# v times p of two pairs in one run, five p buffers, and the third W_out tile behind the attention units

## The chip, the cores and the metric

The kernel runs on one core of a Trainium2 chip. The metric is device microseconds of one execution. Its engines are TensorE (PE, matmuls; PEld is its weight load), VectorE (DVE), ScalarE (ACT), GpSimd (POOL) and SyncE (SP), whose queue issues all of this kernel's DMAs.

## What is computed

Attention with a block-causal mask (8 batches, 8 heads, 576 positions, head size 64), and behind it a feed-forward network on the 4608 tokens:

```python
scores = scale * np.matmul(q, k.transpose(0, 1, 3, 2))
scores = np.where(block_i >= block_j, scores, -1e9)          # blocks of 64
attn = np.exp(scores - scores.max(-1, keepdims=True))
attn = attn / (attn.sum(-1, keepdims=True) + 1e-09)
x = np.matmul(attn, v).transpose(0, 2, 1, 3).reshape(4608, 512)
h = x @ w_in                                                 # 512 x 2048
out = (h * (1.0 / (1.0 + np.exp(-h)))) @ w_out               # 2048 x 512
```

## The kernel before

Most products are made of fp32r pieces, a high part and a low part of each operand, three matmuls for one. v times p alone is in plain fp32, which the trace shows as two matmuls for each one in the program.

The program has three stages. In the first (to about 80 us) the weights W_in arrive as 64-bit words and are turned into numbers, and the first 128 positions of each head are attended to. In the second stage 64 **units** u0 to u63 (8 batches of 8 heads) attend to the other 448 positions, while the first layer of the network (tiles h) runs between them. In the third (from about 620 us) 72 **items** i0 to i71 carry the second layer, each as seven products of sums of blocks, with W_out in the same form.

A unit i has these steps. `load`, `split_hi` (ACT), `split_k`, `split_q` (POOL): q and k in two parts. `scores` (PE, L719): ten matmuls into three of four PSUM banks S. `max`, `gather`, `top`, `spread`, `wide` (DVE and ACT): the maximum of each row. `sub` (DVE, S minus maximum into tile T) and `exp` (ACT, T into tile p). `add` (POOL) and `sums` (DVE): row sums. For each **pair** of units, at the odd one: `sums_x`, `sums_g`, `sums_m`, `inverse` (the factor of each row), `pv` (PE, L824, v times p into PSUM tile U: five widths, two units, ten matmuls in the program and twenty in the trace), `mult` (DVE, U times the factor, into xu), `x_hi` (ACT, L833) and `x_lo` (POOL, L836): the two parts of x, which the first layer reads.

The first layer is cut into **h steps** (`ffn`, six matmuls each, L1063). Two steps fill one tile h, of which there are two buffers; `keep` (ACT, L1069) copies it to SBUF as g, and `save` (SP) writes it to DRAM, from where the items read it again. An h tile can only be begun when the keep of the tile two before it has been done. The h steps of a batch need x of all of its units.

W_out is made of eight tiles t0 to t7, each from two loads o (o0 and o1 for t0, and so on). For one tile: two `load`s into os0 and os1, two `rebias` (ACT, L531, into the tile wraw), three `bits` for each half (DVE, through PSUM bank C, back into wraw), `x` 0 to 2 (POOL, sums and differences into xs), `hi` 0 to 3 (ACT, L646) and `lo` 0 to 3 (POOL, L651). wraw, xs and C have one buffer each. Tiles t0 to t2 (NTA = 3) have room of their own in the pool `ta` and are made while the units run; t3 to t7 stand in room that the units leave free, and are made between the last unit (`all.attended`) and the items.

The order is written out by hand as a list of steps (ORDER): each engine carries out its own instructions in the order of that list, and the semaphores come from the tiles. The list is no time table; only the order on each engine counts.

The lines that the change touches:

```python
def place(u):                                    # of a W_out tile
    if u.d < NTA:
        t = pools["ta"].tile(...)
    elif u.d < 6:
        t = sp.tile([P, 2 * 7 * 256], F32R, tag=f"tb{u.d}", name="tb")
...
n = u.i % 5 if u.double else u.i % 3             # exp: which p buffer
u.p = (pools["p"] if n > 2 else sp).tile([P, COLS], F32, tag=f"p{n}", name="p")
...
for y in (units[u.i - 2], u) if u.double else (u,):       # pv
    U = y.U = (bank("C") if u.double and y is u else pU.tile(...))[:, :NQ]
    for n, (j, c, q0, w) in enumerate(SEG[i] for i in PV):
        for e, z in enumerate((y.mate, y)):
            nc.tensor.matmul(U[64 * e : 64 * e + 64, q0 : q0 + w], y.vv[:, e, j], z.p[:, c : c + w], ...)
```

Of the kernel before, what the change touches and what calls it, by code (L numbers as in the profile page):

```python
# [95 lines left out]
o2.load u0.wide u0.sub:0 u0.sub:1 u1.scores u1.max:0 t0.hi:2 o3.load o2.rebias u3.load keep o3.rebias keep u1.max:1 u0.load_v
u2.split_hi u1.max:2 u1.gather ffn o2.bits:0 u2.split_q save ffn u2.split_k u0.sub:2 u1.top o2.bits:1 t0.lo:2 u1.spread o2.bits:2
keep ffn save u0.exp:0 u1.load_v u1.wide u0.exp:2 ffn u1.sub:0 u1.sub:1 u1.exp:0 u2.scores u1.exp:1 u1.sub:2 save u1.exp:2
u2.max:0 u0.exp:1 u0.add:0 u0.add:1 u3.split_hi u3.split_k u2.max:1 u2.max:2 u2.gather u1.pv u0.sums:0 ffn o3.bits:0 ffn
u3.split_q save u2.top u0.sums:1 u2.spread u1.sums:0 u2.wide u4.load u5.load u2.sub:0 t0.hi:3 u2.sub:1 u2.exp:0 u1.add:0 keep  # L100
u1.add:1 u3.scores u2.exp:1 u4.split_hi u3.max:0 u3.max:1 ffn t0.lo:3 u2.sub:2 keep u3.max:2 u1.sums:1 u4.split_k u4.split_q
u3.gather u1.sums_x u2.exp:2 u1.sums_g u3.top o3.bits:1 ffn o3.bits:2 u3.spread u1.sums_m keep u3.wide u3.sub:0 u3.sub:2 ffn
u3.exp:0 ffn u1.inverse u6.load u2.add:0 ffn u2.add:1 ffn u3.exp:2 save u3.sub:1 u2.sums:0 u4.scores t1.x:0 u1.mult u3.exp:1
u2.sums:1 u4.max:0 u4.max:1 t1.hi:0 u3.add:0 u3.add:1 u3.sums:0 u3.sums:1 t1.hi:2 u2.load_v u3.load_v u4.max:2 keep u5.split_hi
u3.pv u3.sums_x ffn save u4.gather save o4.load t1.lo:0 keep ffn u4.top save u4.spread u4.load_v u5.split_k ffn save keep save
u6.load_v u5.split_q t1.lo:2 u7.load_v u3.sums_g u4.wide u7.load ffn u3.sums_m u4.sub:0 u4.sub:2 u4.exp:0 ffn u1.x_hi u5.load_v
u4.sub:1 u4.exp:2 keep u4.add:0 u3.inverse o5.load u4.exp:1 save u5.scores u3.mult u4.add:1 u5.max:0 u3.x_hi u4.sums:0 ffn u3.x_lo
u6.split_hi u4.sums:1 t1.hi:1 u5.max:1 t1.x:1 ffn u5.max:2 keep u6.split_k save u5.gather ffn u5.top u5.spread ffn keep u5.wide
t1.x:2 u6.split_q u8.load t1.lo:1 u5.sub:0 t1.hi:3 ffn save u5.sub:2 u5.exp:0 t1.lo:3 u5.sub:1 u5.exp:2 u6.scores keep u5.add:0
u6.max:0 u5.exp:1 save u6.max:1 o4.rebias u5.pv u5.add:1 u7.split_hi u6.max:2 u5.sums:0 u7.split_q u5.sums:1 u6.gather u6.top  # L110
u5.sums_x ffn u7.split_k o4.bits:0 u6.spread u8.load_v u9.load_v u6.wide u5.sums_g ffn u6.sub:0 u1.x_lo u9.load u5.sums_m u6.sub:2
u6.sub:1 u7.scores o5.rebias u6.exp:0 u6.exp:2 keep u7.max:0 u6.add:0 u6.exp:1 u7.max:1 save ffn u8.split_hi u6.add:1 u7.max:2 ffn
u8.split_q u5.inverse u7.gather u7.top u6.sums:0 u7.spread u8.split_k ffn u6.sums:1 keep u7.wide save u7.sub:0 ffn u10.load
u7.sub:2 u7.exp:0 u7.sub:1 u7.exp:2 u8.scores keep u8.max:0 u7.add:0 u7.exp:1 save u8.max:1 ffn u9.split_hi u5.mult u7.add:1
u7.sums:0 u7.sums:1 u7.pv u9.split_q u5.x_hi u7.sums_x u8.max:2 u7.sums_g u9.split_k o4.bits:1 u8.gather u8.top ffn u11.load
u5.x_lo o4.bits:2 u8.spread u8.wide t2.hi:0 u10.load_v u7.sums_m ffn u8.sub:0 u11.load_v keep u8.sub:2 u8.exp:0 save ffn u8.sub:1
u8.exp:2 t2.lo:0 u7.inverse u8.exp:1 u8.add:0 u9.scores u7.mult keep u9.max:0 u8.add:1 save u7.x_hi u9.max:1 ffn u10.split_hi
u7.x_lo u9.max:2 ffn u10.split_k u8.sums:0 u9.gather u8.sums:1 u9.top o5.bits:0 ffn u9.spread u10.split_q u9.wide keep ffn
u9.sub:0 save u12.load u9.sub:2 u9.exp:0 u9.sub:1 u10.scores u9.exp:2 keep u10.max:0 u9.add:0 u9.exp:1 u10.max:1 save u9.pv
u11.split_hi u10.max:2 u9.add:1 u11.split_q u9.sums:0 u10.gather u9.sums:1 u10.top u9.sums_x ffn u10.spread u11.split_k o5.bits:1  # L120
u12.load_v u9.sums_g u13.load_v u10.wide u10.sub:0 ffn u13.load u9.sums_m u10.sub:2 u10.exp:0 ffn u10.sub:1 u10.exp:2 keep
u9.inverse u10.add:0 u10.exp:1 u11.scores save u11.max:0 u10.add:1 u11.max:1 ffn u12.split_hi u11.max:2 ffn keep u12.split_q
u10.sums:0 u10.sums:1 u11.gather save u9.mult ffn u12.split_k u11.top u11.spread o5.bits:2 ffn u9.x_hi u11.wide u14.load t2.x:0
keep u11.sub:0 t2.hi:1 ffn save u11.sub:2 u11.exp:0 u9.x_lo t2.hi:2 u11.sub:1 u12.scores u11.exp:2 t2.lo:2 u12.max:0 u11.exp:1
u12.max:1 keep u11.pv u13.split_hi u11.add:0 save u11.sums:0 u12.max:2 u11.add:1 u12.gather u13.split_q u11.sums:1 ffn u14.load_v
u11.sums_x u12.top u15.load_v u12.spread u13.split_k ffn u11.sums_g u12.wide u12.sub:0 u15.load u11.sums_m ffn u12.exp:0 u12.sub:1
keep u12.sub:2 u13.scores u12.exp:1 save u13.max:0 t2.lo:1 u12.exp:2 u13.max:1 ffn u14.split_hi u12.add:0 u13.max:2 ffn keep
u12.sums:0 u11.inverse u13.gather save ffn u13.top u12.add:1 u11.mult u14.split_q u13.spread u14.split_k u11.x_hi u12.sums:1 ffn
keep u13.wide save ffn u13.sub:0 u11.x_lo u16.load u13.sub:1 u13.exp:0 u14.scores u13.sub:2 t2.x:1 u13.exp:1 u13.exp:2 u14.max:0
t2.x:2 u14.max:1 keep u13.pv u13.add:0 u15.split_hi save u14.max:2 u13.add:1 t2.hi:3 u13.sums:0 u14.gather u15.split_q ffn u14.top  # L130
u13.sums:1 u16.load_v u13.sums_x u14.spread u17.load_v u15.split_k u13.sums_g u14.wide ffn u14.sub:0 u17.load u13.sums_m u14.sub:1
u14.exp:0 u15.scores keep u15.max:0 u14.exp:1 save u15.max:1 ffn t2.lo:3 u16.split_hi u15.max:2 ffn u16.split_q u13.inverse
u15.gather u15.top ffn u15.spread u16.split_k u14.sub:2 keep ffn u14.exp:2 u13.mult u15.wide save u13.x_hi u18.load u15.sub:0
u14.add:0 ffn u15.sub:1 u15.exp:0 u13.x_lo keep u15.sub:2 u15.exp:1 u16.scores save u14.sums:0 u15.exp:2 u14.add:1 u16.max:0
u16.max:1 u15.pv u17.split_hi u14.sums:1 u16.max:2 u15.add:0 u15.sums:0 u16.gather u17.split_q ffn u18.load_v u16.top u16.spread
u19.load_v u15.add:1 u16.wide ffn keep u17.split_k u15.sums:1 save u15.sums_x ffn u16.sub:0 u15.sums_g u16.sub:1 u19.load
u16.exp:0 u15.sums_m u17.scores u16.sub:2 u16.exp:1 u16.exp:2 u17.max:0 u17.max:1 ffn keep u16.add:0 u18.split_hi save u17.max:2
u16.sums:0 ffn u16.add:1 u15.inverse u17.gather u18.split_q ffn u17.top u15.mult u17.spread keep u18.split_k u16.sums:1 ffn
u15.x_hi u17.wide save u17.sub:0 ffn u20.load u15.x_lo keep u17.sub:1 u17.exp:0 save u17.sub:2 u18.scores u17.exp:1 u18.max:0
u17.exp:2 u18.max:1 u17.add:0 u17.pv u19.split_hi u18.max:2 u17.add:1 u17.sums:0 u18.gather u19.split_q u17.sums:1 u18.top ffn  # L140
u17.sums_x u20.load_v u18.spread u19.split_k u21.load_v u17.sums_g u18.wide ffn keep u18.sub:0 u21.load u17.sums_m u18.sub:1
u18.exp:0 u19.scores u18.sub:2 save u18.exp:1 u19.max:0 u18.exp:2 ffn u19.max:1 u20.split_hi u18.add:0 u19.max:2 ffn keep
u20.split_q u18.sums:0 u19.gather save u17.inverse ffn u18.add:1 u19.top u17.mult u19.spread u20.split_k ffn u18.sums:1 keep
# [1142 lines left out]
```

## Time and profile before

| | us |
|---|---|
| median of 3 runs | 970.33 |
| lowest and highest run | 970.29, 970.47 |
| the profiled execution | 971.3 |
| its span, first to last instruction | 969.5 |

The page of the profile gives the busy time of each engine over the span, the span in 40 slices of 24.2 us, and the chain of work that ended last. A timeline lists instructions by their start; neighbours of one kind are merged into a row with a count, and a bracket at its end gives the idle time before it and what ended that. Matmuls overlap in the pipeline, so the distance of two starts is their price and not the duration in the row.

### The profile page before, as it was taken

What the parts mean: (1) busy time and instruction counts of PE and PEld (TensorE: products, weight loads), DVE (VectorE), ACT (ScalarE), POOL (GpSimd) and SP (SyncE); (2) the same over time, 40 slices, a digit from 0 to 9 for tenths busy, and PEclk for the clock granted to TensorE, in tenths of its full rate; (3) what the DMA queues carried; (4) which work ended last, traced back from release to release, by engine and by line L of the source; (5) the groups of instructions that cost most, each with busy time, mean ns of one, the idle gap of its engine ahead of it and who ended that gap; (6) DMA issues with size and microseconds to landing.
All of it is one profiled execution on the core that took longest, in us unless ns stands there. A gap on an engine that the chain in (4) does not pass through costs nothing.

```text
span 969.5 us, 20758 instructions
## 1 busy us (share of the span) xinstructions
PE 960.0 (99%) x6922; PEld 869.0 (90%) x6922; DVE 767.5 (79%) x1975; ACT 687.7 (71%) x1557; POOL 619.0 (64%) x724
## 2 busy tenths in 40 slices
PE   8999999999999999999999999999999999999998
PEld 7778778888888888888888899999999999999998
DVE  6868889899999999899999743498877787777762
ACT  5977677777777777777787645799677777677750
POOL 6566897988878778788787647655444444434440
PEclk9999999999999999999999999999999999999999
DMA  9956655555555555455555166665454454444521
GB/s 345 360 187 192 193 162 156 150 152 157 146 157 154 150 159 159 137 157 163 142 157 161 68 203 200 199 185 156 122 165 137 135 158 129 136 140 137 139 66 45
DMA packets 109803, 155.51 MB, mean 160 GB/s; under 512 B 18560, under 2 KB 83072, under 8 KB 109696
## 3 DMA queue, kind: packets, MB, share of 16 engines
q1 hardware_dynamic: 109696, 154.18, 53.6%
q8 instruction: 55, 0.90, 0.4%
q14 instruction: 52, 0.43, 0.1%
HBM read 106.95 MB, written 47.19 MB: 159 GB/s over the span
## 4 chain that ended last, share of the span: by engine, by line
PE 95%; DMA 2%; ACT 1%; DVE 1%; SPq 0%; POOL 0%; issue 0%; ACTq 0%; POOLq 0%
PE h L1063 40%; PE S L1140 25%; PE c L1140 10%; PE S L719 9%; PE U L824 9%; DMA v<-in_v_dram 2%; PE S L1004 1%; PE S L881 0%; PE S L1035 0%; ACT raw L1091 0%; DVE Mx L658 0%; POOL MR L874 0%; ACT gc L1124 0%; SPq L905 0%; PE h L853 0%
## 5 line engine op out<-in xcount | busy, mean ns | idle before, releaser
L1063 PE MATMUL h<-x,wi 128*128 128x448 f32 (+2 forms) x1968 | 416.8, 367 | 0.0
L1063 PEld LDWEIGHTS h<-x,wi 128*128 128x128 f32 x1968 | 356.8, 188 | 34.1 <-issue 0.7
L658 DVE TRANSPOSE_TENSOR_REDUCE Mx<-S 64x4 f32<-64x128 f32 (+4 forms) x384 | 130.5, 400 | 8.9 <-PE S L719 8.0
L773 ACT ACTIVATE p<-T 128x512 f32<-128x512 f32 (+1 forms) x192 | 115.0, 614 | 26.9 <-DVE T L762 20.1
L1069 ACT COPY g<-h 128x448 f32<-128x448 f32 (+1 forms) x160 | 86.3, 539 | 36.4 <-PE h L1063 22.0
L1128 POOL TENSOR_TENSOR x<-raw,x 128x512 fp32r<-128x512 f32 (+1 forms) x58 | 59.3, 1027 | 72.9 <-ACT x L1124 59.9
L779 POOL TENSOR_TENSOR pa<-p 128x448 f32<-128x448 f32 x64 | 73.7, 1151 | 43.7 <-ACT p L773 37.9
L1128 POOL TENSOR_TENSOR wi<-raw,wi 128x512 fp32r<-128x512 f32 (+1 forms) x56 | 57.3, 1027 | 67.9 <-ACT wi L1124 58.6
L700 POOL TENSOR_TENSOR qh<-qk,qh 64x576 fp32r<-64x576 f32 x64 | 91.8, 1434 | 6.4 <-POOL xs L636 0.8
L719 PE MATMUL S<-qh 128*128 128x448 f32 (+3 forms) x320 | 92.2, 301 | 0.1
L824 PE MATMUL U<-p,v 128*64 128x448 f32 (+3 forms) x640 | 87.0, 416 | 0.4 <-DMA v<-in_v_dram 0.4
L719 PE MATMUL S<-ql,qh 128*128 128x448 f32 (+3 forms) x320 | 83.9, 306 | 0.0
L694 ACT CAST qh<-qk 128x1024 fp32r<-128x1024 f32 x64 | 67.0, 1047 | 22.5 <-PE S L719 5.9
L704 POOL TENSOR_TENSOR ql<-qk,qh 128x448 fp32r<-128x448 f32 x64 | 73.7, 1151 | 14.0 <-issue 6.7
L824 PEld LDWEIGHTS U<-p,v 128*64 128x64 f32 x640 | 44.0, 136 | 41.0 <-issue 29.0
L1091 ACT ACTIVATE raw<-raw 128x1024 f32<-128x1024 f32 x72 | 76.6, 1064 | 0.0
L765 DVE TENSOR_TENSOR T<-S,MR 128x128 f32<-128x128 f32 (+2 forms) x192 | 73.4, 409 | 0.0
L719 PEld LDWEIGHTS S<-ql,qh 128*128 128x128 f32 (+1 forms) x320 | 56.9, 178 | 6.4
L719 PEld LDWEIGHTS S<-qh 128*128 128x128 f32 (+1 forms) x320 | 56.8, 178 | 3.6 <-issue 0.3
L782 POOL TENSOR_TENSOR pa<-pa,p 128x320 f32<-128x320 f32 x64 | 55.9, 874 | 5.3 <-ACT p L773 1.5
L744 ACT COPY m<-m 32x14 f32<-32x14 f32 x192 | 38.7, 202 | 23.9 <-DVE m L740 22.2
L1128 POOL TENSOR_TENSOR gc<-raw,gc 128x512 fp32r<-128x512 f32 (+1 forms) x30 | 30.8, 1031 | 37.0 <-ACT gc L1124 30.1
(198 smaller groups left out, 2065.9 us busy)
## 6 DMA issues: line engine op xcount, KB each, us to landing
qk<-in_qk_dram SPq DMA_DIRECT2D x128, 256.0 KB, 3.8
gdb<-g SPq DMA_DIRECT2D x128, 224.0 KB, 2.4
raw<-gdb SPq DMA_DIRECT2D x64, 256.0 KB, 3.2
v<-in_v_dram SPq DMA_DIRECT2D x64, 160.0 KB, 2.3
wst<-in_moe_w_in_dram SPq DMA_DIRECT2D x16, 512.0 KB, 8.4
wst<-in_moe_w_out_dram SPq DMA_DIRECT2D x16, 512.0 KB, 4.4
gd<-g SPq DMA_DIRECT2D x32, 256.0 KB, 3.7
raw<-gd SPq DMA_DIRECT2D x32, 256.0 KB, 3.5
```

Source lines behind the costliest of these rows:

```text
L658: nc.vector.tensor_reduce(out=out, in_=in_, axis=AX.X, op=op, apply_transpose=True)
L700: nc.gpsimd.tensor_tensor(out=u.qh[r, c], in0=u.raw[r, c], in1=u.qh[r, c], op=ALU.subtract)
L704: nc.gpsimd.tensor_tensor(out=u.ql, in0=u.raw[:, :NQ], in1=u.qh[:, :NQ], op=ALU.subtract)
L719: nc.tensor.matmul(u.ps(c, w, m), u.kk[r, j * P : j * P + m], q[r, q0 : q0 + w], start=qq == 0 and not (ROWS and seg == 2), stop=qq == 1 a ...
L773: nc.scalar.activation(u.p[:, c:e], u.T[:, c:e], AF.Exp, scale=SCALE)
L779: nc.gpsimd.tensor_tensor(out=u.pa, in0=u.p[:, :NQ], in1=u.p[:, 960 : 960 + NQ], op=ALU.add)
L824: nc.tensor.matmul(U[64 * e : 64 * e + 64, q0 : q0 + w], y.vv[:, e, j], z.p[:, c : c + w], start=n == 0, stop=n == 4)
L1063: nc.tensor.matmul(o, wi[wt][:, c, w], x_of(g, c, xt), start=c + k == 0, stop=c == CT - 1 and k == 2)
L1069: nc.scalar.copy(g, hs.pop(z)[:, :n])
L1091: nc.scalar.activation(u.raw, u.raw, AF.Silu)
L1128: e.tensor_tensor(out=u.goal(1, k), in0=u.source(k), in1=u.goal(0, k), op=ALU.subtract)
L1140: nc.tensor.matmul(o, quarter(u.g[a], j)[:, P * e : P * e + P], quarter(turned[d].g[b], TORDER[FACTOR[pr]]), start=u.q == 0 and i % 2 == 0 ...
```

## The change

Two constants and the order list are changed:

```diff
-NTA = 3
-DOUBLE = 0
+NTA = 2
+DOUBLE = 1
...
-u62.sub:2 u63.gather u61.inverse u62.exp:2 ffn keep u63.top u62.add:0 u61.mult u63.spread save u62.sums:0 ffn u61.x_hi u63.wide
...
+u63.exp:1 u63.add:0 u59.x_hi u63.add:1 save ffn u63.sums:0 ffn u63.sums:1 u63.sums_x keep u63.pv u61.inverse ffn u59.x_lo u61.mult
```

With DOUBLE = 1, units from u8 on rotate through five p buffers, two of them in a pool of their own that takes the place of the third tile of `ta`. pv is called for every fourth unit (u11, u15, up to u63) and carries out two pairs, the earlier one into U and the later one into bank C. Before, pv ran 32 times, once for each pair; now 4 times for one pair and 14 times for two. With NTA = 2 the tile t2 belongs to the tiles in the units' room, and stands behind `all.attended` with t3 to t7: six tiles are made there, and five were. The list is another from about the first unit to the place where t6 is finished; from there to the end (from o14, through all items) it is the same, step for step. The lines of the changed file stand one lower in number (L823 for L824, L530 for L531).

PE at the first pair of batch 1 (units u8 and u9; S are scores, U is v times p, h the first layer), before:

```order
L719 MATMUL S0_2315<-ql_2290,qh_2256 64x64
L824 MATMUL U_2337<-p_2205,v_1973 64x448
L824 MATMUL U_2337<-p_2308,v_1973 64x448
L824 MATMUL U_2337<-p_2205,v_1973 64x448
L824 MATMUL U_2337<-p_2308,v_1973 64x448
L824 MATMUL U_2337<-p_2205,v_1973 64x320
L824 MATMUL U_2337<-p_2308,v_1973 64x320
L824 MATMUL U_2337<-p_2205,v_1973 64x192
L824 MATMUL U_2337<-p_2308,v_1973 64x192
L824 MATMUL U_2337<-p_2205,v_1973 64x64
L824 MATMUL U_2337<-p_2308,v_1973 64x64
L1063 MATMUL h_2367<-x_81,wi0_78 128x448 x2
```

and PE at the same pair and the next one (u10 and u11) now; the rows begin with the end of the first pair:

```order
L823 MATMUL U_2440<-p_2242,v_2098 64x64
L823 MATMUL SC_2451<-p_2289,v_2200 64x448
L823 MATMUL SC_2451<-p_2406,v_2200 64x448
L823 MATMUL SC_2451<-p_2289,v_2200 64x448
L823 MATMUL SC_2451<-p_2406,v_2200 64x448
L823 MATMUL SC_2451<-p_2289,v_2200 64x320
L823 MATMUL SC_2451<-p_2406,v_2200 64x320
L823 MATMUL SC_2451<-p_2289,v_2200 64x192
L823 MATMUL SC_2451<-p_2406,v_2200 64x192
L823 MATMUL SC_2451<-p_2289,v_2200 64x64
L823 MATMUL SC_2451<-p_2406,v_2200 64x64
L1062 MATMUL h_2492<-x_81,wi0_78 128x448 x2
```

The second pair follows the first without scores or h between them.

ACT at the end of the last unit (p is the last exp, g are keeps, x is x_hi, wraw is a rebias, dj belongs to the row sums), before:

```order
L1069 COPY g_7757<-h_7717 128x448
L667 COPY dj_7771<-dj_7771 32x28 x3
L1069 COPY g_7797<-h_7763 128x448
L1069 COPY g_7818<-h_7790 128x448
L833 CAST x_81<-xu_7809 128x448
L1069 COPY g_7844<-h_7811 128x448
L1069 COPY g_7860<-h_7837 128x448
L531 ACTIVATE wraw_7862<-wst_7833 128x512
L1069 COPY g_7881<-h_7853 128x448
L531 ACTIVATE wraw_7862<-wst_7835 128x512
L646 CAST tb_7894<-wraw_7862 128x256
```

and now:

```order
L832 CAST x_81<-xu_7710 128x448
L1068 COPY g_7739<-h_7721 128x448
L666 COPY dj_7737<-dj_7737 32x28 x3
L832 CAST x_81<-xu_7774 128x448
L832 CAST x_81<-xu_7800 128x448
L530 ACTIVATE wraw_7820<-wst_7816 128x512
L1068 COPY g_7825<-h_7766 128x448
L530 ACTIVATE wraw_7820<-wst_7818 128x512
L645 CAST tb_7854<-wraw_7820 128x256
```

The first rebias (now o4's, then o6's) stands right behind the last x_hi, where two keeps stood between them. On PE the last run of v times p stands four h steps later in the program than it did.

ACT at the rebias of o12, the first of the tile t6 (tb are hi of t5, then wi0 is hi of t6), before:

```order
L1069 COPY g_8132<-h_8108 128x448
L646 CAST tb_8089<-xs_8104 128x512
L531 ACTIVATE wraw_8151<-wst_8087 128x512
L1069 COPY g_8154<-h_8125 128x448
L1069 COPY g_8174<-h_8144 128x448
L531 ACTIVATE wraw_8151<-wst_8106 128x512
L646 CAST wi0_78<-wraw_8151 128x256
```

and now:

```order
L1068 COPY g_8107<-h_8088 128x448
L530 ACTIVATE wraw_8141<-wst_8080 128x512
L645 CAST tb_8082<-xs_8105 128x512
L1068 COPY g_8147<-h_8112 128x448
L530 ACTIVATE wraw_8141<-wst_8109 128x512
L645 CAST tb_8082<-xs_8105 128x512
L1068 COPY g_8159<-h_8128 128x448
L645 CAST wi0_78<-wraw_8141 128x256
```

The two casts of t5 now stand behind the rebias, and each has a keep behind it.

## Rows read from the trace of the kernel before

**Rows 1.** The page: busy time of the engines, the granted TensorE clock in 40 slices (tenths of full speed), and the shares of the chain that ended last.

```profile
PE 960.0 (99%) x6922; PEld 869.0 (90%) x6922; DVE 767.5 (79%) x1975; ACT 687.7 (71%) x1557; POOL 619.0 (64%) x724
...
PEclk9999999999999999999999999999999999999999
...
PE 95%; DMA 2%; ACT 1%; DVE 1%; SPq 0%; POOL 0%; issue 0%; ACTq 0%; POOLq 0%
```

**Rows 2.** Who waited for whom, PE alone, the whole span: us in total, times, longest. These two are the only ones behind the first stage.

```profile
PE U L824 <- DMA v<-in_v_dram: 0.4, 1, 0.4
PE S L1140 <- DVE x L1128: 0.4, 1, 0.4
```

**Rows 3.** Timeline of PE at pairs in the middle of the units (start, us, engine, line, operation, tiles, shape, count); each row is of an answer for a stretch so narrow that it shows single matmuls.

```profile
301.72 2.57 PE L1063 MATMUL h<-x,wi 128*128 128x448 f32 x12
304.12 0.36 PE L719 MATMUL S<-qh 128*128 128x448 f32 x1
...
305.47 0.22 PE L719 MATMUL S<-ql,qh 128*64 128x64 f32 x1
305.62 0.60 PE L824 MATMUL U<-p,v 128*64 128x448 f32 x2
306.05 0.55 PE L824 MATMUL U<-p,v 128*64 128x448 f32 x2
306.42 0.55 PE L824 MATMUL U<-p,v 128*64 128x448 f32 x2
306.80 0.55 PE L824 MATMUL U<-p,v 128*64 128x448 f32 x2
...
308.05 0.28 PE L824 MATMUL U<-p,v 128*64 128x64 f32 x3
308.10 0.22 PE L824 MATMUL U<-p,v 128*64 128x64 f32 x1
308.25 0.48 PE L1063 MATMUL h<-x,wi 128*128 128x448 f32 x1
308.57 0.36 PE L1063 MATMUL h<-x,wi 128*128 128x448 f32 x1
...
312.13 0.22 PE L719 MATMUL S<-ql,qh 128*64 128x64 f32 x1
312.19 0.45 PE L1063 MATMUL h<-x,wi 128*128 128x448 f32 x1
312.48 0.57 PE L1063 MATMUL h<-x,wi 128*128 128x448 f32 x2
```

**Rows 4.** Timelines of PE, DVE, ACT, POOL and SP at the end of the last unit, and the page's row on the loads of W_out (issues, KB of each, median us from issue to landing).

```profile
552.24 2.70 PE L824 MATMUL U<-p,v 128*64 128x448 f32 x20
554.88 11.47 PE L1063 MATMUL h<-x,wi 128*128 128x448 f32 x56
...
559.48 0.62 DVE L828 TENSOR_TENSOR xu<-U,MR 128x448 f32<-128x448 f32 x1
...
560.59 0.57 ACT L833 CAST x<-xu 128x448 fp32r<-128x448 f32 x1
...
565.26 0.67 ACT L531 ACTIVATE wraw<-wst 128x512 f32<-128x512 f32 x1
...
wst<-in_moe_w_out_dram SPq DMA_DIRECT2D x16, 512.0 KB, 4.4
```

**Rows 5.** Timelines of ACT, DVE and POOL along W_out tiles behind the units: t5 from its first rebias to the first one of t6, then the end of t6 and the first rebias of t7.

```profile
586.86 1.23 ACT L531 ACTIVATE wraw<-wst 128x512 f32<-128x512 f32 x2
587.57 0.69 DVE L554 TENSOR_SCALAR SC<-wraw 128x512 uint32<-128x512 uint32 x1 [6.97 <-ACT wraw L531]
591.35 0.69 DVE L564 SCALAR_TENSOR_TENSOR wraw<-wst,SC 128x512 uint32<-128x512 uint32 x1
592.18 1.29 POOL L632 TENSOR_TENSOR xs<-wraw 128x512 f32<-128x512 f32 x1 [1.14 <-DVE wraw L564]
595.06 1.29 POOL L651 TENSOR_TENSOR tb<-wraw,tb 128x512 fp32r<-128x512 f32 x1
596.39 0.67 ACT L531 ACTIVATE wraw<-wst 128x512 f32<-128x512 f32 x1 [0.63 <-POOL tb L651]
...
605.92 0.62 ACT L646 CAST wi<-xs 128x512 fp32r<-128x512 f32 x1 [1.72 <-POOL xs L636]
606.45 0.53 ACT L1069 COPY g<-h 128x448 f32<-128x448 f32 x1
606.87 1.23 ACT L531 ACTIVATE wraw<-wst 128x512 f32<-128x512 f32 x2
```

**Rows 6.** Timelines of POOL and PE where the items begin.

```profile
619.59 2.01 POOL L1128 TENSOR_TENSOR gc<-raw,gc 128x512 fp32r<-128x512 f32 x2 [0.71 <-ACT gc L1124]
...
620.99 1.58 PE L1140 MATMUL S<-ta,gc 128*128 128x256 f32 x12
...
628.37 0.39 PE L1140 MATMUL S<-ta,x 128*128 128x256 f32 x2
629.12 0.38 PE L1140 MATMUL S<-ta,x 128*128 128x256 f32 x1 [0.35 <-DVE x L1128]
```

**Rows 7.** Busy time by engine in stretches (us; PE, PEld, DVE, ACT, POOL with their instructions; granted clock, DMA share, GB/s).

```profile
300.00:450.00 150.00, 150.00 (x864) 128.44 (x863) 138.26 (x411) 111.44 (x286) 120.72 (x154) 1.00 0.54 151
...
575.00:600.00 25.00, 25.00 (x127) 23.43 (x126) 10.85 (x16) 13.76 (x26) 16.91 (x17) 1.00 0.58 176
```

More of the change, by code (lines that the diff above doesn't have):

```diff
@@ L96 @@
[L96 to L143, printed above, removed]
@@ L148 @@
-keep u19.inverse u21.gather save u22.split_q ffn u19.mult u21.top u20.sums:0 u21.spread u22.split_k u20.sums:1 ffn u19.x_hi
-u21.wide keep u24.load u19.x_lo u21.sub:0 ffn u21.sub:1 u21.exp:0 save u21.sub:2 u22.scores u21.exp:1 u21.exp:2 u22.max:0
-u22.max:1 keep u21.pv u21.add:0 u23.split_hi save u22.max:2 u21.add:1 u21.sums:0 u22.gather u23.split_q u21.sums:1 ffn u22.top
-u21.sums_x u24.load_v u22.spread u23.split_k u25.load_v u21.sums_g u22.wide ffn u22.sub:0 u25.load u21.sums_m u22.sub:1 u22.exp:0
@@ new lines @@
+u16.add:0 ffn u15.sums_m u17.sub:2 u18.top u18.spread keep u15.inverse u16.sums:0 u19.split_k u13.x_hi u11.x_lo save u19.split_q
+u18.wide ffn u16.add:1 u18.sub:0 u15.mult save u17.exp:0 u17.exp:1 u18.sub:1 u19.scores ffn u15.x_hi keep u13.x_lo u17.exp:2
+u21.load u18.sub:2 u19.max:0 u17.load_v u16.sums:1 ffn u20.split_hi keep u19.max:1 u19.max:2 u15.x_lo u19.gather u20.split_k
+u19.top u19.spread u20.split_q u18.exp:0 u19.wide u19.sub:0 u18.exp:1 u19.sub:2 ffn u19.sub:1 ffn ffn u20.scores u19.exp:0
@@ new lines @@
+u20.add:1 ffn u23.top keep ffn u24.split_k u19.inverse u23.spread u22.load_v u22.exp:2 ffn u21.sums:0 save u23.wide u23.sub:0
+u24.split_q u23.sub:2 u23.sub:1 u20.sums:1 u19.mult u23.exp:0 u17.x_lo u21.load_v u25.load keep u21.add:0 u24.scores u23.exp:2
+u21.add:1 u24.max:0 u25.split_hi u24.max:1 u23.exp:1 u23.load_v u22.exp:1 u24.max:2 u21.sums:1 u23.pv save u24.gather u21.sums_x
+ffn keep u25.split_k u21.sums_g u24.top u24.spread u25.split_q save u19.x_hi u24.wide u24.sub:0 u24.sub:1 u21.sums_m u25.scores
@@ new lines @@
+u23.sums_x u26.sub:0 u26.sub:1 keep save u25.exp:2 u27.split_q u23.sums_g u24.sums:0 u26.exp:0 u21.mult save u27.scores u27.max:0
+u24.add:0 u27.max:1 u21.x_hi ffn u23.sums_m u27.load_v ffn u24.add:1 u28.split_hi save keep u27.max:2 ffn u27.gather keep ffn ffn
+u24.sums:1 u26.sub:2 u27.top u23.inverse save u27.spread u27.wide u28.split_q u29.load u23.mult u25.exp:1 u27.sub:0 t1.hi:3
+u27.sub:1 u26.exp:1 u27.exp:0 u27.exp:1 u28.split_k u28.scores u21.x_lo u28.max:0 u25.add:0 u26.exp:2 u28.max:1 u28.max:2
```

362 lines of the change are left out of this document (200 added, 162 removed).

## The prediction

> **What bounds the kernel now.** I read the page first: PE is busy for 99% of the span, the clock is at its upper level in every slice, and 95% of the chain that ended last is PE [rows 1]. Then who PE waited for: behind the first stage there are two waits of 0.4 us, and none at all from 110 us until the items begin at 621 us [rows 2, 6]. So between the units the time is the sum of PE's own matmuls, and only two things count: matmul time that goes, and waits of PE that come. The third view is PE's timeline at the pairs, single matmuls [rows 3]: it shows what a run of v times p costs beside its arithmetic. The fourth is what ACT, DVE and POOL do between the last unit and the items [rows 4 to 6], since the change puts a sixth W_out tile there.
>
> The sums are made in the profiled execution (971.3 us, span 969.5). The median is 0.97 us below it; a difference found in the trace is added to the median as it is.
>
> **Fewer runs of v times p.** The distance of two starts is the price of a matmul. Twelve h matmuls take 304.12 - 301.72 = 2.40 us, 0.20 each [rows 3], a step of six 1.20. At the edges of a run more is paid [rows 3]:
> - scores to U: 305.47 to 305.62 is 0.15, and the first pair of 448 wide rows takes 0.43 where the next take 0.37: 0.21 with both.
> - U to h: 308.10 to 308.25 is 0.15, and the first h takes 0.32 and not 0.20: 0.27.
> - scores to h without a run: 0.06, and the first h takes 0.29: 0.15.
>
> I counted the edges in the order of both. Scores to U go from 30 to 17 (-13 x 0.21 = -2.7 us), U to h from 32 to 13 (-19 x 0.27 = -5.1), scores to h from 34 to 47 (+13 x 0.15 = +2.0). Five runs are now followed by scores; no row shows that edge. Its bounds are 0.15 and 0.27, the two edges into fp32r pieces; I take 0.27, that of U (+1.4). One h-to-U edge goes (-0.1). Fourteen times a second pair now follows a first one inside a run, which no row shows either. The low end is 0.05, the distance of two narrow pairs of one run (308.05 to 308.10); the high end is the two edges that a new run pays, 0.21 + 0.27 = 0.48. The nearest row is the low one, since kind, width and weights are alike: 14 x 0.05 = +0.7. The sum is -3.8 us; with the high ends it is +2.2 and with the low one for the five scores -4.4. [...]
>
> The matmuls themselves, and every instruction of ACT, DVE and POOL, stay in number. Were nothing else to happen, the time would be 966.5.
>
> **The sixth W_out tile.** Before, t2 was made beside the units at no cost to PE [rows 2]. Now its 2 loads, 2 rebias, 6 bits, 4 hi, 3 sums and 4 lo stand behind the last unit, ahead of t3 on each queue. What a tile costs there: the first rebias at 586.86, the bits of both halves on DVE until 592.04, the sums and the wide lo on POOL from 592.18 to 596.35, and the next tile's first rebias at 596.39, which sat idle for that POOL lo [rows 5]: wraw has one buffer. That is a closed circle of 9.53 us, and no engine in it can start earlier, though none is full (POOL 16.9 of 25 us, [rows 7]). From t6 to t7 it is 606.87 - 596.39 = 10.48, since the last hi and a keep stand ahead of the rebias (605.92, 606.45) [rows 5]; they still do.
>
> When can it start? Behind the last x_hi. Before, PE's last U run began at 552.24 and h went on at 554.88 [rows 4]. Now that run is one pair longer and stands 24 h matmuls (4.8 us) later, and PE is 3.8 earlier: U is ready at 554.9 + 4.8 - 3.8 = 555.9. Add mult 0.62 and x_hi 0.57 [rows 4]: first rebias at 557.2, where it was at 565.26. Its load stands on SP behind the save of an h tile that is finished ahead of the U run (551), so with 4.4 us to landing [rows 4] it is there by 557.
>
> From there t7's first rebias is four circles and the long one away: 557.2 + 4 x 9.53 + 10.48 = 605.8. It was at 606.87. PE however comes 3.8 us earlier, and from this rebias on the list is unchanged: before, the first lo of an item ended about 620.6 and PE used it at 620.99, 0.4 us later, and at 628.4 PE waited for an item's DVE part [rows 6]. So there is no slack to take up the difference: the items begin when the W_out chain lets them. **Of 3.8 us gained only 1.1 remains, if the chain runs without a stop: 969.2.**
>
> It will not quite. PE needs a keep for each h tile, and ACT's keeps stand between the rebias in a fixed order. Nineteen keeps lie between the first rebias and t7's, 45.6 us of h steps, against 48.6 of chain, so PE must stop. The worst place is t6: a keep that stood right behind o12's rebias now has a cast of t5 ahead of it as well, and the keep before that stands ahead of the rebias. The rebias comes at 557.2 + 4 x 9.53 = 595.3; rebias 0.67, cast 0.62 and keep 0.53 [rows 5], whose starts overlap a little, end about 596.9; and PE, which without stops wants that buffer 30 steps behind the U run, at 555.9 + 30 x 1.20 = 591.9, has by then lost 5.0 us. It then needs 8 steps (9.6) for the tile whose keep stands ahead of t7's rebias: 596.9 + 9.6 = 606.5, the keep 0.5 and its wait 0.2: 607.2. By this, t7 starts 0.4 us later than before, and PE enters the items 0.4 to 0.8 us later: 970.7. I count on this end, as the order on ACT is fixed, and forecast **970.6**, no change that can be measured. What a measurement can tell from no change is about 0.2%, 1.9 us.
>
> **Rivals.**
> 1. *The gain stands (966.5).* The chain would have to reach t7's rebias at 606.9 - 3.8 = 603.1, in 45.9 us instead of 48.6, 0.5 less for each tile. That could come from a shorter circle where POOL's lo and sums stand in another order. Against it: with the other order, 596.39 to 605.92 (where ACT sat idle for POOL), the circle was as long [rows 5]. To leave the range of no change, half of that would do. Chance 0.13.
> 2. *PE stops among the units (slower).* DVE is busy for 138.3 of 150 us there [rows 7], and a run of two pairs keeps PE from making scores or h for 5.1 us. Moreover the pair's x comes late: in before x_lo stood at least two h steps ahead of the batch's first use (2.4 us); now at u15, u21, u23, u31 and u55 it stands zero or one step ahead. From xu to x it takes mult 0.62, x_hi 0.57 and x_lo 1.15, 2.3 us, plus what stands ahead on POOL. If PE waits half a microsecond for x or for a score bank at each of the seven batches, that is +3.5 us, all of it ahead of the W_out chain, whose start moves along: 974.1. It decides from 0.3 us a batch on (2 us in all). For it speaks that DVE has 8% left; against it, that at the same load PE did not wait once in before. Chance 0.27.
> 3. *The second pair pays like a new run* (0.48 for 0.05): PE gains nothing, but then U is ready 6 us later, the chain ends at 611.8, and the time is some 975. A part of rival 2's range; chance within it 0.03.
>
> **How the numbers follow.** The forecast 0.60: 969.2 to 972.0, with small stops among the units. Slower by over 0.2% 0.27 (rivals 2 and 3), faster by over 0.2% 0.13 (rival 1). The range leaves out most of the first rival and the far end of the second: 968.4 to 973.6.
>
> **What would show it.** Right: the runs of U of 40 matmuls with one edge each; first rebias behind the units near 557 us; distances of the tiles' first rebias of 9.5 us; PE idle before h for ACT's keep (g) between 577 and 600 us, in sum about 5 us; t7's rebias at 606 to 607; the items starting within a microsecond of 621. Wrong: a rebias distance under 9.2 us, or no waits of PE there (rival 1); waits of PE for POOL's x or for DVE before 550 us (rival 2); more than 0.1 us between the pairs inside a run (rival 3).

## The result and the profile after

| | kernel before | changed kernel |
|---|---|---|
| time, median | 970.33 us (970.09 to 970.71) | 976.4 us (973.69 to 977.23) |
| profiled execution | 971.3 us, span 969.5 | 977.23 us, span 975.5 |
| last run of v times p ends (PE goes on with h) | 554.88 us | 559.88 us |
| items begin on PE | 620.99 us | 627.43 us |

The change makes the kernel slower by about half a percent: the ratio is 1.0052, 95% interval 1.004 to 1.0064, or 3.9 to 6.2 us. (One further execution, of 3372 us, is left out of the range and the ratio; the median counts it, and is 976.1 without it.) The forecast was 970.6, and the time lies outside its range. The items take 348.1 us (975.5 - 627.43), and took 348.5 (969.5 - 620.99); what is lost is lost ahead of them.

The page after, busy time of PE, granted clock in 40 slices and shares of the chain that ended last [rows 1]:

```profile
PE 962.4 (99%) x6922; PEld 868.8 (89%) x6922; DVE 766.8 (79%) x1975; ACT 680.7 (70%) x1557; POOL 617.1 (63%) x724
...
PEclk9999999999999999999999999999999999999999
...
PE 88%; DVE 3%; POOL 3%; DMA 2%; ACT 2%; issue 1%; SPq 0%; DVEq 0%; POOLq 0%; ACTq 0%
```

PE's share of the chain has fallen from 95% to 88%, and DVE and POOL have come in with 3% each, for 1% and 0% (DMA stays at 2%): a part of the time now runs through the W_out tiles. Who PE waited for, whole span (us, times, longest), the rows that are new or bear on what follows [rows 2]:

```profile
PE h L1062 <- ACT g L1068: 3.0, 3, 2.1
...
PE S L1034 <- ACT MR L883: 0.9, 1, 0.9
...
PE SC L823 <- DMA v<-in_v_dram: 0.2, 1, 0.2
```

The first is the keep behind the units. The second is c2's v times p in the first stage. The third lies in a merged run. There is no wait for POOL's x and none in the items.

PE's timeline at one merged run and what follows it [rows 3] (answers for narrow stretches; U is the first pair's bank, SC the second's):

```profile
434.60 0.22 PE L718 MATMUL S<-ql,qh 128*64 128x64 f32 x1
434.75 0.97 PE L823 MATMUL U<-p,v 128*64 128x448 f32 x4
...
437.28 0.92 PE L823 MATMUL SC<-p,v 128*64 128x448 f32 x4
...
439.86 0.47 PE L718 MATMUL S<-qh 128*128 128x448 f32 x1
440.17 0.36 PE L718 MATMUL S<-ql,qh 128*128 128x448 f32 x1
```

Both pairs take 439.86 - 434.75 = 5.11 us. One pair alone takes 308.25 - 305.62 = 2.63 with its exit [rows 3], two 5.26, which is 0.15 more. The second pair begins 437.28 - 434.75 = 2.53 behind the first, and one pair takes 308.10 - 305.62 = 2.48 to its last matmul [rows 3], so the boundary costs 0.05, the low end. Scores behind a run: the first one takes 0.31 and the next 0.21.

Behind the units, PE (start, us, operation, count, idle before and who ended it):

```profile
554.77 2.70 PE L823 MATMUL U<-p,v 128*64 128x448 f32 x20
557.30 2.65 PE L823 MATMUL SC<-p,v 128*64 128x448 f32 x20
559.88 21.88 PE L1062 MATMUL h<-x,wi 128*128 128x448 f32 x108
582.30 5.08 PE L1062 MATMUL h<-x,wi 128*128 128x448 f32 x24 [0.54 <-ACT g L1068]
587.84 10.63 PE L1062 MATMUL h<-x,wi 128*128 128x448 f32 x48 [0.45 <-ACT g L1068]
600.52 27.06 PE L1062 MATMUL h<-x,wi 128*128 128x448 f32 x126 [2.06 <-ACT g L1068]
627.43 1.56 PE L1139 MATMUL S<-ta,gc 128*128 128x256 f32 x12
```

and ACT, each W_out tile's first rebias, with the worst keep between:

```profile
561.22 0.66 ACT L530 ACTIVATE wraw<-wst 128x512 f32<-128x512 f32 x1
...
570.58 0.67 ACT L530 ACTIVATE wraw<-wst 128x512 f32<-128x512 f32 x1 [1.56 <-POOL tb L650]
...
580.09 0.67 ACT L530 ACTIVATE wraw<-wst 128x512 f32<-128x512 f32 x1 [1.82 <-POOL tb L650]
...
589.48 0.67 ACT L530 ACTIVATE wraw<-wst 128x512 f32<-128x512 f32 x1 [1.70 <-POOL xs L635]
...
598.87 0.66 ACT L530 ACTIVATE wraw<-wst 128x512 f32<-128x512 f32 x1 [3.13 <-POOL xs L635]
599.44 0.60 ACT L645 CAST tb<-xs 128x512 fp32r<-128x512 f32 x1
599.95 0.53 ACT L1068 COPY g<-h 128x448 f32<-128x448 f32 x1
...
612.50 1.22 ACT L530 ACTIVATE wraw<-wst 128x512 f32<-128x512 f32 x2
```

The circle (from a tile's first rebias round to the next one's) is there: 9.36, 9.51, 9.39 and 9.39 us. The keep that lets PE go on at 600.52 stands behind o12's rebias and a cast. The 306 h matmuls between 559.88 and 627.43 take 67.55 us; in a run below that does not stop they take 61.32. Of the 6.2 us between, 126 x 0.2004 = 25.25 against 627.43 - 600.52 = 26.91 leaves 1.7 behind the last stop, and 4.6 are the stops (3.05 of it is idle time in the records, the rest longer distances of starts). Where the 1.7 are is seen in two rows, the fourteen matmuls behind the stop, 4.66 us to the end of the last, where fourteen distances of 0.20 are 2.8, and the stretch's granted clock:

```profile
600.52 4.66 PE L1062 MATMUL h<-x,wi 128*128 128x448 f32 x14 [2.06 <-ACT g L1068]
...
600.00:620.00 20.00, 19.48 (x89) 18.08 (x90) 7.88 (x12) 10.03 (x21) 12.63 (x13) 0.91 0.52 168
```

Ahead of the last run, PE is 4.0 us later than forecast (559.88 for 555.9). The places are in 160 to 196 us and in two merged runs. SP and ACT in the first place, then PE and SP at u43's and u59's run:

```profile
159.05 1.11 SPq L682 DMA_DIRECT2D qk<-in_qk_dram  x2
167.85 0.34 SPq L689 DMA_DIRECT2D v<-in_v_dram  x1
168.28 1.24 SPq L1073 DMA_DIRECT2D gdb<-g  x1
169.61 1.12 SPq L682 DMA_DIRECT2D qk<-in_qk_dram  x2
...
176.26 6.38 SPq L1073 DMA_DIRECT2D gdb<-g  x3
182.69 0.42 SPq L689 DMA_DIRECT2D v<-in_v_dram  x1
183.21 2.39 SPq L682 DMA_DIRECT2D qk<-in_qk_dram  x4
...
174.11 1.05 ACT L693 CAST qh<-qk 128x1024 fp32r<-128x1024 f32 x1 [2.30 <-DMA qk<-in_qk_dram]
...
188.91 1.05 ACT L693 CAST qh<-qk 128x1024 fp32r<-128x1024 f32 x1 [1.24 <-DMA qk<-in_qk_dram]
...
401.60 0.58 SPq L689 DMA_DIRECT2D v<-in_v_dram  x1
...
405.13 3.17 PE L823 MATMUL SC<-p,v 128*64 128x448 f32 x20
...
524.76 0.92 PE L823 MATMUL SC<-p,v 128*64 128x448 f32 x2
525.86 2.67 PE L823 MATMUL SC<-p,v 128*64 128x448 f32 x18 [0.19 <-DMA v<-in_v_dram]
```

At 160 us SP stands for 7.6 us before a load of v: its buffer is free only when the first merged run has used it, since two pairs are now used at once. Behind it stand a save and the loads of q and k; ACT's split waits 2.3 us for them, and later 1.2 behind three saves; ACT's and DVE's work is late, and PE waits for score banks and keeps in pieces of 0.1 to 0.3 us, seen as longer distances of starts. At u43 and u59, SP issues the load of the second pair's v some 3.4 us before that pair is due (405.13, 524.76), behind loads of q and k that wait for their buffer. These two places are no accident of one execution: in the six profiles below and above that have these loads where the changed kernel has them (with one wraw or two, with and without t2's work) the runs there take 5.4 to 5.6 and 5.7 to 6.6 us, and in the five with the loads moved 5.1.

### The profile page after: what moved, and what is told of

Its sections match the earlier page's. It is cut to its first block, busy times and chain, and to the rows that moved or that the text cites. A ratio compares the mean times of both kernels' runs of the same rounds, so it can differ in the third digit from the quotient of the medians.

```text
span 975.5 us, 20744 instructions
## 1 busy us (share of the span) xinstructions
PE 962.4 (99%) x6922; PEld 868.8 (89%) x6922; DVE 766.8 (79%) x1975; ACT 680.7 (70%) x1557; POOL 617.1 (63%) x724
## 4 chain that ended last, share of the span: by engine, by line
PE 88%; DVE 3%; POOL 3%; DMA 2%; ACT 2%; issue 1%; SPq 0%; DVEq 0%; POOLq 0%; ACTq 0%
PE h L1062 35%; PE S L1139 25%; PE c L1139 10%; PE S L718 9%; PE U L823 5%; PE SC L823 4%; DMA qk<-in_qk_dram 1%; DMA wst<-in_moe_w_in_dram 1%; DVE SC L557 1%; DVE SC L553 1%; DVE wraw L563 1%; PE S L1003 1%; POOL xs L631 1%; POOL tb L650 1%; DMA v<-in_v_dram 0%
## 5 line engine op out<-in xcount | busy, mean ns | idle before, releaser
L772 ACT ACTIVATE p<-T 128x512 f32<-128x512 f32 (+1 forms) x192 | 112.9, 611 | 13.4 <-DVE T L761 8.6
L764 DVE TENSOR_TENSOR T<-S,MR 128x256 f32<-128x256 f32 (+2 forms) x192 | 73.1, 408 | 0.0
L1139 PE MATMUL S<-tb,x 128*128 128x256 f32 x450 | 56.1, 276 | 0.0
L661 DVE STREAM_TRANSPOSE MR<-m 128x448 f32<-128x448 f32 x64 | 40.7, 636 | 17.7 <-ACT m L743 16.5
L1139 PEld LDWEIGHTS S<-tb,x 128*128 128x128 f32 x450 | 53.3, 188 | 0.1
```

The lines of the kernel that those rows point to most:

```text
L772: nc.scalar.activation(u.p[:, c:e], u.T[:, c:e], AF.Exp, scale=SCALE)
L1139: nc.tensor.matmul(o, quarter(u.g[a], j)[:, P * e : P * e + P], quarter(turned[d].g[b], TORDER[FACTOR[pr]]), start=u.q == 0 and i % 2 == 0 ...
```

## The experiments

Each time stands beside the kernel before on the same chip (970.5 to 970.6); ratios carry 95% intervals. Two theories stood at the start. Theory 1: the circle and the keeps behind it cost the time behind the units. Theory 2: the time is lost among the units, and behind them PE's stops are free.

**A second wraw buffer.**

```diff
-u.w = sp.tile([P, 4, 256], F32, tag="wraw", name="wraw")
+u.w = (
+    sp.tile([P, 2 * 7 * 256 + 5 * SHIFT], F32, tag="gc", name="wraw2")[:, :1024].rearrange("p (n m) -> p n m", n=4)
+    if u.d in (2, 4, 6) else sp.tile([P, 4, 256], F32, tag="wraw", name="wraw")
+)
```

> The changed kernel with a second wraw buffer for t2, t4 and t6 (in the space that the items' gc takes later); same order, same arithmetic. Theory 1 (behind the units the one wraw closes a circle of 9.4 us per tile, ACT's keeps stand behind rebias and casts in it, PE stops 4.0 us for them and then runs ten matmuls at 373 ns for 201): the distance of the tiles' first rebias falls from 9.4 to at most 8.5 us, PE stops under 1 us there, the clock stays at 1.0, the items begin near 621.5 us instead of 627.4, and the time falls by 5 to 6 us to about 971. Theory 2 (what is lost lies among the units, about 4 us, and behind them the items begin when the W_out chain lets them, so that PE's stops there cost nothing by themselves): under 2 us of change, 974.5 to 976.5.

Measured: 979.45, ratio 1.0088 (1.0074 to 1.0103). Half of theory 1 came true: PE made its 306 h without a stop and the items began at 620.70. But they took 357.0 us, and not 348.1. Matmuls of the items by form, 640 to 940 us (count, busy us, mean ns), of this run:

```profile
L1142 PE MATMUL S<-tb,x 128*128 128x256 f32 x360 | 46.5, 281 | 0.0
...
L1142 PE MATMUL S<-ta,x 128*128 128x256 f32 x210 | 26.2, 277 | 0.0
```

and of the changed kernel:

```profile
L1139 PE MATMUL S<-tb,x 128*128 128x256 f32 x360 | 44.7, 276 | 0.0
L1139 PE MATMUL S<-ta,x 128*128 128x256 f32 x210 | 26.1, 276 | 0.0
```

Only those with a tb tile are clearly slower. The new buffer had moved all four in SBUF (the first from byte 114048 to 124608). So this run did not decide.

**Keeps of ACT ahead** (PE's and ACT's steps at the worst place).

```diff
-t5.hi:1 keep ffn ffn ffn ffn o12.rebias t5.hi:2 keep ffn o13.rebias t5.hi:3 keep
+keep t5.hi:1 ffn ffn keep ffn ffn keep o12.rebias ffn ffn keep t5.hi:2 o13.rebias t5.hi:3
```

> The changed kernel with twelve ACT keeps of h behind the units put ahead of the rebias or cast that they stood behind (each no earlier than its h tile is finished); nothing else moved but six h steps that had to be written ahead of them. Theory 1: the circle stays at 9.4 us per tile, but PE finds a free h bank each time: stops under 1 us, no stretch of slow matmuls, items near 621.5 to 623 us, time 970.5 to 972.5. Theory 2 (the W_out chain and not PE sets the start of the items): items stay at 626 to 627.5, time 975 to 976.5, PE only waits later, ahead of the items.

Measured: 977.4, 1.0067 (1.0055 to 1.0079). A miss for theory 1, as made. PE still waited 4.1 us, since ACT now waited itself: g has three buffers, and the saves that free them stood on SP behind W_out loads.

```profile
600.17 0.53 ACT L1068 COPY g<-h 128x448 f32<-128x448 f32 x1 [4.69 <-DMA gdb<-g]
```

**The moved tile alone**, without merged runs.

```diff
-NTA = 3
+NTA = 2
-u4.gather save o4.load t1.lo:0 keep
+u4.gather save t1.lo:0 keep
-u63.x_lo all.attended o6.load o7.load
+u63.x_lo all.attended ffn o4.load o5.load o4.rebias
```

> The kernel before, its units as they were (one pair in a run of v times p, three p buffers), but with W_out tile t2 moved behind the units, and the order behind the units that of the changed kernel. Theory 1: the moved tile costs by itself nearly all that is lost: stops of PE of about 4 us and the slow matmuls behind them, 975 to 976.5. Theory 2 (the merged runs cost the time among the units, and the moved tile little): 970 to 972.

Measured: 979.55, 1.0092 (1.0079 to 1.0105): this version costs 9 us, more than theory 1 said. PE waited 5.9 us in five stops for the keep, the clock of 600 to 620 us was again 0.91, and the items began at 629.65. Two of the five stops, 1.10 and 1.61 us ahead of 564.54 and 573.92, are not in the changed kernel; they stand just behind the place where the old order of the units meets the new one, so not all of the 9 us is the tile's.

**Without the tile's work.**

```diff
+turned[2].g = turned[1].g
...
-ffn o4.load o5.load o4.rebias o4.bits:0 o4.bits:1 keep o4.bits:2 o5.rebias o5.bits:0 ffn save o6.load
+ffn keep ffn save o6.load
```

> The changed kernel without the work of W_out tile t2: its loads, rebias, bits, sums, casts and lows are left out, and the items use t1's tiles in its place, so the output lacks that tile's part. Units and everything else as in the changed kernel. Theory 1: no stop of PE behind the units, items near 621.5, 970 to 971.5; it would be 966.5 if the merged runs gained their 3.8 us, and the 4 us lost among units and first stage keep it at 970 to 971. Theory 2 (the tile costs little): 974.5 to 976.5.

Measured: 973.07 (972.36 to 976.7), 1.0033 (1.002 to 1.0046). Between the theories, and the design was weak: the keeps ahead of t3's steps in the list now held ACT, t3's first rebias came at 569.37 and o12's at 598.37, where it was, so the stop of 2.05 us stayed. This is read from the profiled execution, the slowest of six (976.7), 3.6 us above the median; its mean granted clock is 0.998 and that of the five others 1.000, so the slow matmuls that it shows behind the stop are not theirs, and whether they have the stop is not shown.

**Two wraw buffers, all tiles at their places.** As the first experiment, and

```diff
 pools["work"] = tc.alloc_tile_pool(name="end", bufs=1, reuse_waits="tile")
+for tag, n in (("os0", 1024), ("os1", 1024), ("wraw", 1024), ("tb2", 3584), ("xs", 1024), ("tb3", 3584), ("tb4", 3584), ("tb5", 3584)):
+    pools["work"].tile([P, n], F32, tag=tag, name="room")
```

> The changed kernel with the second wraw buffer as in the run before of that kind, but the W_out tiles, sums, first wraw and gc keep the SBUF places that they have in the changed kernel. In the run before of that kind PE did not stop behind the units and the items began at 620.7 us (627.4 in the changed kernel), yet the items' matmuls started every 117 ns and not every 113, and three of its W_out tiles lay at other places. Theory 1 (the circle costs 5.7 us behind the units; the slower items came from the places): items begin near 621 us, items' matmuls at 113 ns, time 970 to 972. Rival (an earlier start of the items itself makes them slower, by the transfers or the engines that they meet): matmuls stay at 117 ns and the time at 978 to 980.

Measured: 970.38, 0.9998 (0.9989 to 1.0007), as theory 1 said. The items' matmuls are back at 113 ns from start to start, so the places were the first run's trouble. PE behind the units:

```profile
559.02 61.48 PE L1065 MATMUL h<-x,wi 128*128 128x448 f32 x306
620.34 1.58 PE L1142 MATMUL S<-ta,gc 128*128 128x256 f32 x12
```

The tiles' first rebias came at 560.36, 568.01, 576.61, 584.20 and 591.49: 7.3 to 8.6 us for 9.4.

**Four steps moved ahead of and among the units.**

```diff
-c2.pv c2.hi c2.lo ffn u0.load_v u0.scores
+ffn c2.pv c2.hi c2.lo u0.load_v u0.scores
-u12.spread u12.load_v u12.wide
+u12.spread u12.wide
-keep u13.load_v u14.sub:1
+keep u12.load_v u13.load_v u14.sub:1
-u46.load u43.sub:1 u43.load_v u43.exp:0
+u43.load_v u46.load u43.sub:1 u43.exp:0
-u62.load ffn u58.exp:2 u60.scores u53.x_lo u59.exp:1 u60.max:0 u59.load_v
+u59.load_v u62.load ffn u58.exp:2 u60.scores u53.x_lo u59.exp:1 u60.max:0
```

> The changed kernel with four steps moved in the order ahead of and among the units, nothing behind them: one h step ahead of c2's v times p; u12's load of v behind eight loads and saves that it kept waiting on SP; u43's and u59's load of v ahead of a load of q and k that waits for its buffer. Theory 1 (most of the 4 us lost ahead of and among the units are a wait of 1.0 for c2's x, waits of some 1.3 in 176 to 196 us behind the late loads of q and k, and the 1.6 us in which the second pair's v comes late): the last U run ends at 557 us for 559.9, time 2 to 3.5 us less than the changed kernel, 973 to 974.5. Rival (the merged runs themselves keep PE from scores, and DVE is late with the score banks): under 1 us, 975.4 to 977.

Measured: 975.33, 1.0051 (1.0039 to 1.0064), 1.1 us less than the changed kernel, and not told apart from it (1.004 to 1.0064): a miss for theory 1. The two late runs were clean, but the moved h step left u0's scores to wait for c2's bank:

```profile
PE S L718 <- DVE x L1042: 1.5, 1, 1.5
...
600.22 25.47 PE L1062 MATMUL h<-x,wi 128*128 128x448 f32 x126 [2.05 <-ACT g L1068]
```

The second row is PE behind the units: the stop is that of the changed kernel, but the 126 matmuls behind it take 25.47 us and not 27.06, 0.201 from start to start up to the items at 625.53.

**Both together.** The two diffs above.

> The moves among the units and the second wraw buffer in its place together. Theory 1: the two parts add up, 967 to 969, and the merged runs show most of their 3.8 us. Rival (what is gained among the units is taken back behind them, since the W_out chain sets the start of the items): 970 to 972, PE waiting ahead of or in the first items.

Measured: 970.58, 0.9999 (0.999 to 1.0008): nothing beyond the second buffer. That fits the rival, yet PE did not wait in or ahead of the items; it lost 1.5 us at u0's scores and 1.6 near 192 us, before the last run. So the rival's time came by another way.

**Keeps and saves ahead, one wraw.** The keeps as above, and each save right behind its keep:

```diff
-t5.hi:1 t5.x:0 keep o13.load t5.lo:1 ffn t5.x:1 t5.x:2 ffn save ffn ffn o12.rebias
+t5.hi:1 ffn ffn keep save t5.x:0 o13.load t5.lo:1 t5.x:1 t5.x:2 ffn ffn keep save o12.rebias
```

> The changed kernel with one wraw, twelve keeps of ACT behind the units put ahead of the rebias or cast that they stood behind, and every save of these h tiles right behind its keep, ahead of the W_out loads that it stood behind on SP. With the keeps alone ahead, ACT waited for the saves of g (4.7 us ahead of one keep). Theory 1 (PE's stops come from the order of keeps and saves around the circle, not from the length of the circle): PE stops under 1.5 us in sum behind the units, no slow matmuls, time 971 to 973.5. Rival (a circle of 9.4 us per tile for W_out sets the items' start however the keeps stand): items not ahead of 625 us, time 975 to 976.5.

Measured: 972.85, 1.0024 (1.0015 to 1.0032), as theory 1 said. PE:

```profile
559.91 58.37 PE L1062 MATMUL h<-x,wi 128*128 128x448 f32 x288
618.67 4.27 PE L1062 MATMUL h<-x,wi 128*128 128x448 f32 x18 [0.39 <-ACT g L1068]
622.77 0.40 PE L1139 MATMUL S<-ta,gc 128*128 128x256 f32 x2
```

The circle is as long (570.63, 580.14, 589.54, 598.96), yet the items begin 4.7 us earlier. So with one buffer it is the order of keeps and saves around the circle that stops PE, and the chain of tiles alone does not set the items' start at 627.

**Units again, with and without the steps at c2** (both with two wraw in place). Added to the three loads of v, and in the first of the two runs the steps at c2:

```diff
-u14.gather save u11.add:1 ffn ffn u14.top
+u14.gather u16.load save u11.add:1 ffn ffn u14.top
-u15.max:1 u16.load u15.max:2
+u15.max:1 u15.max:2
-c2.pv c2.hi c2.lo ffn u0.load_v u0.scores keep o2.rebias ffn
+ffn c2.pv c2.hi c2.lo u0.load_v keep ffn u0.scores o2.rebias
```

> Two wraw buffers in place, and the units mended again: one h step ahead of c2's v times p and, since that step was missed ahead of u0's scores (PE waited 1.5 us there for c2's bank), one more h step and its keep ahead of these; the three loads of v moved as before; and u16's load of q and k ahead of the three saves behind which it stood on SP (ACT waited 2.2 us for its data, PE 1.6 us in 192 to 196). Theory 1 (the stops ahead of and among the units are late loads and one order of steps, not the merged runs): last U run ends near 556 us for 559.0 with two wraw alone, PE without a wait behind, time 966.5 to 968.5, faster than the kernel before. Rival (what is gained there comes back as another wait of the same chain, DVE's score banks or the W_out chain): 969.5 to 971.

> As the run beside it, without the two moved h steps at c2 and u0's scores: two wraw buffers, three loads of v moved, u16's load ahead of three saves. Theory 1: the loads are worth about 2.5 us among the units (0.5 at u43, 0.6 at u59, some 1.5 between 175 and 197 us), so 967.5 to 969; the run beside it is 0.5 to 1.2 us faster. Rival: 970 to 971, as with two wraw alone.

Measured: 968.66, 0.9979 (0.9971 to 0.9988), and without the steps at c2 967.3, 0.9964 (0.9952 to 0.9977). The loads are worth 3.1 us; the steps at c2, expected to save 0.5 to 1.2, cost 1.4. PE in the faster one:

```profile
403.64 2.65 PE L826 MATMUL SC<-p,v 128*64 128x448 f32 x20
...
522.77 2.65 PE L826 MATMUL SC<-p,v 128*64 128x448 f32 x20
...
556.78 61.48 PE L1065 MATMUL h<-x,wi 128*128 128x448 f32 x306
618.10 1.58 PE L1142 MATMUL S<-ta,gc 128*128 128x256 f32 x12
```

The second pairs at u43 and u59 are clean, and the last run ends at 556.78. This version beats both kernels: 3.3 us under the kernel before.

**The moved tile alone, two wraw in place.** The third and the fifth experiment's diffs.

> The kernel before with its units as they were and t2 behind them in the order of the changed kernel, now with two wraw buffers in place. Theory 1 (the tile costs because of the one wraw): the stops of 0.7, 0.5 and 2.1 us and the slow matmuls behind the last of them go; the two of 1.1 and 1.6 us near 564 and 573 us, for keeps behind casts of u63's x, may stay: 971 to 974 for the 979.5 with one wraw. If the merged runs gained nothing at all, this and the changed kernel with two wraw (970.4) would differ only by these two stops. Rival (the tile's work itself costs, by DVE, POOL or the transfers): 976 to 979.

Measured: 972.67, 1.002 (1.0011 to 1.0029), 6.9 us less than with one wraw: most of the price was the one buffer and not the tile's work. 2.1 us are left. Two stops stayed, at 564 and 583 us, 1.26 and 0.41 us of idle in the records; the first stands behind a rebias that waited 3.7 us for its load.

**The loads alone, one wraw.** The four loads moved, nothing else.

> The changed kernel with one wraw, and only the four loads moved: u12's, u43's and u59's load of v, and u16's load of q and k ahead of three saves. With two wraw these moves were worth 3.1 us (967.3 for 970.4). Theory 1 (behind the units nothing sets an absolute time: the tile circle starts when u63's x_hi is done, and moves along): the two mends add up, 972.5 to 974 for the changed kernel's 976.4. Rival (the one wraw takes back what the units gain, since the start of the items hangs on the tiles): 975.5 to 976.5, and longer stops of PE behind the units.

Measured: 973.52, 1.0031 (1.0019 to 1.0042). The parts add: 976.4 - 973.5 = 2.9 and, with two wraw, 970.4 - 967.3 = 3.1. Behind the units the picture of the changed kernel returns 3.65 us earlier, slow matmuls and all (0.87 of it is there at u1's run of v times p, 90.55 us for 91.42, ahead of every moved step):

```profile
556.23 21.88 PE L1062 MATMUL h<-x,wi 128*128 128x448 f32 x108
...
596.90 27.00 PE L1062 MATMUL h<-x,wi 128*128 128x448 f32 x126 [2.06 <-ACT g L1068]
623.74 1.56 PE L1139 MATMUL S<-ta,gc 128*128 128x256 f32 x12
```

## Why the prediction was wrong

The sum had waits of PE among the units at nothing, and the price of the one wraw too low. In the profiled execution (977.23, where the forecast is 970.6 + 0.97 = 971.6) they are 4.0 us ahead of and among the units, and 1.7 of slow matmuls behind a stop, together 5.7. The medians of the experiments say much the same without a single trace: moving four loads is worth 2.9 and 3.1 us, where the sum had nothing, and the second wraw buffer 6.0 (976.4 to 970.4) and 6.2 (973.5 to 967.3), where the sum had 4.1 (966.5 to 970.6). That is some 5 of the 5.8 us between 970.6 and 976.4; the rest is not placed.

- **What bounds the kernel:** right. Every loss that a trace shows is a wait of PE or a slower PE.
- **Edges, -3.8 us:** right. The edges measured are those of the sum (the U edges, scores to h, the boundary at the low end), scores behind a run cost 0.25 and not 0.27. With both waits taken away the kernel is 3.3 us faster than before, 967.3, where the first rival had 966.5. What makes the edges is not shown: the last scores are printed with 128*64 as U's matmuls are, and the step from them to U costs 0.15 all the same [rows 3].
- **Waits among the units:** the failed step. The forecast had them at "small stops" and left the rest to rival 2, at 0.27. The size of that rival was near (3.5, and 4.0 measured), but by luck, for its causes were not those: PE waited nowhere for x, and DVE's score banks cost six waits of 0.1 to 0.2 us. The cause is two pairs of v in use at once. A buffer of v comes free later and is wanted sooner; its load holds SP, and the loads of q and k behind it. I had priced the merged runs on PE, DVE and POOL, and not on SP, though the change keeps two pairs' v in use at once. The rows give 1.3 us between 165 and 196 us (30.56 from run to run, 29.23 with the loads moved), 0.5 at u43 and 1.1 at u59. Moving four loads gave back 2.9 and 3.1. With the loads moved the last run ends at 556.23 and 556.78, 0.3 to 0.9 behind the forecast. The profiled execution has a wait of 0.9 at c2's v times p in the first stage; of the seven other profiles with the same steps there six list no wait on that line and one 0.4, so most of it is of this execution, and the attempts to mend it were of no use.
- **Start of the W_out chain:** right but for the 4.0 us; the first rebias came 1.34 us behind the last run, forecast 1.3.
- **The circle of 9.53 us:** right (9.36 to 9.51), and that the one buffer of wraw closes it is shown: with two the distance falls to 7.3 to 8.6 and PE does not stop.
- **Keeps behind rebias and cast stop PE by 5.0 us, worst at o12's rebias:** right in place and near in size (4.6, of which the last stop has 2.06 in one piece).
- **"The items begin when the W_out chain lets them":** wrong as a rule. With keeps and saves ahead the items began 4.7 us earlier behind the same circle. t7's rebias at 612.50 waits for keeps of h tiles that PE had not made, so PE sets it. The start is a sum of PE's own parts: 559.88 + 61.3 for the matmuls + 4.6 of stops + 1.7 of slow matmuls = 627.4.
- **Clock:** a term at nothing without a reason. I treated a stop as its own length; the profiled execution pays 1.7 us more, with the granted clock at 0.50 from 601.3 to 604.6 us. (The row PEclk, with 9 for 90% or more of a slice of 24 us, hides so short a stretch.) Not every execution pays: this one has a mean granted clock of 0.998, and those of 973.69, 975.76 and 976.40 have 1.000, so they had no such stretch (3.3 us at 0.50 take 0.0017 off the mean), and what they lost in its place is not shown. A mean of 0.998 does not say where the stretch lies: the profiled execution of the kernel before has 0.998 too, with 0.50 from 15.0 to 18.3 us, a stretch that the 9 of its slice hides [rows 1]. That 970.6 + 4.0 + 1.7 = 976.3 meets the median is luck. With the loads alone moved, six executions of seven have 0.998 (973.38 to 973.75), and the one with 1.000 is the shortest, 972.27.
- **Rival 3** (the second pair pays like a new run): out; 0.05 at the boundary.

Open: the changed kernel spreads over 3.5 us, the kernel before over 0.6 beside it (2.8 over 27 executions later). One execution of each is profiled. In the five runs with the same steps up to the last run of v times p (two wraw at either place, keeps ahead, keeps and saves ahead, without the tile's work) that run ends at 559.02 to 561.38 us, so the 4.0 us of the changed kernel's profile is 3.1 to 5.5 in others.
